# Pooled attention and a max-of-three feed-forward: batch 1's key path and steps placed elsewhere

## The chip, the cores and the metric

The kernel runs on one core of one Trainium2 chip. The metric is the device time of one launch, in microseconds. The core has engines with instruction streams of their own: TensorE (PE in the profile, its weight loads PEld), VectorE (DVE), ScalarE (ACT), GpSimd (POOL) and SyncE (SP). Each works through its own stream in the order in which the program wrote it, and they meet through semaphores. DMA transfers are started from the streams of POOL and SP here.

## The reference

```python
# q, k, v: (8, 8, 576, 64); pool = 8, Sp = 72
k_p = k.reshape(B, H, Sp, pool, D).mean(axis=3)
v_p = v.reshape(B, H, Sp, pool, D).mean(axis=3)
scores = scale * np.matmul(q, k_p.transpose(0, 1, 3, 2))
attn = softmax(scores)                         # over the 72 pooled keys
x = np.matmul(attn, v_p)                       # (8, 8, 576, 64)
x = x.transpose(0, 2, 1, 3).reshape(4608, 512)
h = np.maximum(np.maximum(x @ w1, x @ w2), x @ w3)   # w1, w2, w3: 512 x 768
out = h @ w_out                                      # 768 x 512
```

Keys and values are averaged over groups of eight positions, 576 queries of each head attend to 72 pooled keys, and the result goes through a layer that takes the largest of three products.

## The kernel before

**The arithmetic.** The maximum is taken against the first product: `h = x w1 + max(0, x (w2 - w1), x (w3 - w1))`, so `sub_w` subtracts w1 from w2 and w3 once, and `x w1 wout` becomes one product with `wm = w1 wout`, which `linear` makes once. For it w1 has to stand transposed: `turn_w(jc)` transposes one of six slabs of 128 columns on TensorE (four transposes into the PSUM buffer of the tag `tr`, of which there is one) and copies it to `w1T`.

**The blocks.** The 4608 tokens are done in nine blocks of 512 (`block(n, plan)`), eight batches of 576 tokens feed them. `hidden` makes the hidden layer of a block: for each of six slabs the product with w2-w1 (ScalarE takes the relu into `t`) and the product with w3-w1 (VectorE takes the maximum into `hT`). `project` makes the output: per 128 tokens four matmuls of `xT` with `wm` and six of `hT` with `wout`, a copy `osb` on ScalarE and two stores. In block 0 the product `linear` stands between them: four row slabs of six matmuls, copied to `wm` by VectorE and ScalarE in turn.

**The slots.** `hidden`, `linear` and `project` are generators. After each piece they yield, and `block` then writes the steps that the plan holds for that slot: so the order on TensorE is laid down by hand. Block 0 has 34 slots: 0 to 17 in `hidden`, 18 to 25 in `linear` (one after every three matmuls), 26 to 33 in `project` (an even one after the four matmuls with `wm`, an odd one after the six with `wout`). In block 1, which has no `linear`, slots 0 to 11 come after four matmuls of 256 columns each, 12 to 17 after four of 512, and 18 to 25 are those of `project`.

**The steps of a batch.** `K` or `fold_k` sums eight keys to one (`kp`, each sum twice side by side). `k` is `turn_k`: six transposes of `kp` into PSUM, then two VectorE copies (`fill_kz`) to `kz`, of which there are two, by parity of the batch. `q0` to `q3` transpose four parts of the queries through the buffer `tr` and copy them to `qT` on ScalarE (small letter) or VectorE (capital `Q`). `s0` to `s7` are the heads' scores: three matmuls into one of the two PSUM buffers of the tag `att`, then an exponential on ScalarE. `v0` to `v4` multiply 128 queries of all heads with the pooled values, in an `att` buffer, and VectorE divides. `x0` to `x4` transpose that into `xT`. `w` is `turn_w`, `d` is `sub_w`, and `T` is a DMA that transposes all queries of a batch, from batch 3 on.

**Who folds.** Batch 0's keys and values are folded on VectorE and TensorE in the prologue. From batch 1 on GpSimd folds: `fold_k(b)` halves eight keys to four, four to two, and writes the last sum twice, through a float32 buffer `half`; `fold_v(b)` does the same for the values. GpSimd's stream also starts the loads: behind all weights stand the loads of batch 1 and 2, then `fold_k(1)`, `fold_v(1)`, the loads of batch 3, `fold_k(2)`, `fold_v(2)`, and in each later block the loads of batch n+3 and the folds of batch n+2 (`pool_work`). A load into one of the two buffers of a kind waits until the batch before the last has been read.

**PSUM.** Eight banks: `tr` 1, `pw` 3, `att` 2 of two banks each. The `pw` buffers carry the hidden products, the row slabs of `linear` and the output in turn, so the fourth of a row waits for the first to be read.

**The prologue** (L374 to L450) warms TensorE up with `heat(n)`, n multiplications of 512 columns into `tr` that nobody reads. Single ones stand at L438, L441 and L445 between the last score steps of batch 0.

Of the kernel before, what the change touches and what calls it, by code (L numbers as in the profile page):

```python
# [14 lines left out]
def kernel(  # L15
# [11 lines left out]
    nc = tc.nc  # L27
    dt = mybir.dt
    F32, BF16, F16 = dt.float32, dt.bfloat16, dt.float16

    B, H, S, D = q.shape
# [19 lines left out]
    const = ctx.enter_context(tc.tile_pool(name="const", bufs=1))  # L51
# [6 lines left out]
    kts, vts, qbs, kps, qTs, ets = {}, {}, {}, {}, {}, {}  # L58
# [65 lines left out]
    nc.vector.memset(vp_all[:, :, :, D:65], float(POOL))  # L124
    xT = const.tile([128, KCH, TOK], F16, name="xT", tag="xT")

    def fold(e, t, outs):
        part, n = t.shape[:2]
        f = const.tile([part, n, 4, D], F32, name="half", tag="half")
        e.tensor_tensor(out=f, in0=t[:, :, 0:4, :], in1=t[:, :, 4:8, :], op=ALU.add)  # L130
        e.tensor_tensor(out=f[:, :, 0:2, :], in0=f[:, :, 0:2, :], in1=f[:, :, 2:4, :],  # L131
                        op=ALU.add)
        for o in outs:
            e.tensor_tensor(out=o, in0=f[:, :, 0, :], in1=f[:, :, 1, :], op=ALU.add)  # L134

    def new_kp(b):
        kps[b] = sb2.tile([96, 6, 2, D], BF16, name="kp", tag="kp")

    def fold_k(b, e, i0=0, i1=6):
        if b not in kps:  # L140
            new_kp(b)
        fold(e, kts[b][:, i0:i1], [kps[b][:, i0:i1, i, :] for i in range(2)])

    def fold_v(b):
        fold(nc.gpsimd, vts[b], [vp_all[:, b, :, 0:D]])
# [1 line left out]
    def pool_v(b, h, g, tag, evac):  # L147

        pvp = psp.tile([128, g - h, D], F32, name="pvp", tag=tag[0], bufs=tag[1])
        for j in range(POOL):  # L150
            nc.tensor.matmul(pvp, identh[0:Sp, :], vts[b][:, h:g, j, :],
                             start=(j == 0), stop=(j == POOL - 1))
        evac(out=vp_all[:, b, h:g, 0:D], in_=pvp[0:Sp])

    def turn_q(b, n0, n1, evac, tag):
        if b not in qTs:
            qTs[b] = sb2.tile([128, 2 * NG, 128], BF16, name="qT", tag="qT")
        pqt = psp.tile([128, n1 - n0, 128], BF16, name="pqt", tag=tag[0],
                       bufs=tag[1])
        qf = qbs[b].rearrange("p hp t d -> p (hp t d)")  # L160
        for n in range(n0, n1):
            nc.tensor.transpose(pqt[:, n - n0, :], qf[:, 128 * n:128 * n + 128],  # L162
                                ident)
        evac(out=qTs[b][:, n0:n1, :], in_=pqt)

    def keys(b, tag):
        pkt = psp.tile([128, 6, 96], BF16, name="pkt", tag=tag[0], bufs=tag[1])
        for i in range(6):
            nc.tensor.transpose(pkt[:, i, :], kps[b][:, i, :, :], ident[0:96, 0:96])  # L169
        return pkt  # L170

    def fill_kz(b, par, h0, h1, pkt, evac):
        rows = slice(64 * par, 64 * par + 64)
        evac(out=kz_all[b % 2][rows, par, h0:h1, 0:Sp].rearrange(  # L174
                 "p h (r i) -> p h r i", i=6),
             in_=pkt[rows, :, 12 * h0:12 * h1].rearrange("p i (h r) -> p h r i", r=12))

    def turn_k(b):
        pkt = keys(b, TR)
        for par in range(2):  # L180
            fill_kz(b, par, 0, H, pkt, nc.vector.tensor_copy)

    def pool_k(b, tag):

        new_kp(b)
        pkp = psp.tile([128, 6, D], F32, name="pkp", tag=tag[0], bufs=tag[1])
        for j in range(POOL):
            nc.tensor.matmul(pkp, identh[0:96, :], kts[b][:, :, j, :],
                             start=(j == 0), stop=(j == POOL - 1))
        nc.vector.tensor_copy(out=kps[b][:, :, 0, :], in_=pkp[0:96])  # L190
        nc.scalar.copy(out=kps[b][:, :, 1, :], in_=pkp[0:96])
# [12 lines left out]
    def new_et(b):  # L204
        ets[b] = sb2.tile([Sp, H, S], F16, name="et", tag="et")

    def scores(b, h):
        psc = psp.tile([128, 1024], F32, name="psc", tag="att", bufs=2)
        score(b, h, psc[:, 0:320], 0, 0, 5)
        score(b, h, psc[:, 320:512], 1, 0, 3)  # L210
        score(b, h, psc[:, 512:576], 1, 3, 4)
        exp(ets[b][:, h, :], psc[0:Sp, 0:S])
# [33 lines left out]
    TR = ("tr", 1)  # L246
    PW = ("pw", 3)
# [4 lines left out]
    def do(b, steps):  # L252

        for name in steps.split():
            i = int(name[1:] or 0)
            if name[0] in "qQ":
                turn_q(b, *QS[i], nc.vector.tensor_copy if name[0] == "Q"
                       else nc.scalar.copy, TR)  # L260
            elif name[0] == "T":
                qTs[b] = sb2.tile([128, 2 * NG, 128], BF16, name="qT", tag="qT")
                nc.sync.dma_start_transpose(
                    out=qTs[b], in_=qbs[b].rearrange("p hp t d -> p (hp t d)"))
            elif name[0] == "k":
                turn_k(b)
            elif name[0] == "K":
                pool_k(b, PW)
            elif name[0] == "p":
                pool_v(b, 4 * i, 4 * i + 4, TR, nc.scalar.copy)  # L270
            elif name[0] == "s":
                if i == 0:
                    new_et(b)
                scores(b, i)
            elif name[0] == "d":
                sub_w(i)
            elif name[0] == "w":
                turn_w(i, nc.scalar.copy if i % 2 else nc.vector.tensor_copy)
            elif name[0] == "v":
                xns[b, i] = values(b, CHUNKS[i][0])  # L280
            else:
                turn_x(b, *CHUNKS[i], xns[b, i], ("att", 2),
                       nc.vector.tensor_copy if name[0] == "X" else nc.scalar.copy)
# [4 lines left out]
    def sub_w(i):  # L288

        part = slice(256 * i, 256 * i + 256)  # L290
        for t in w_sb[1:]:
            nc.vector.tensor_tensor(out=t[:, :, part], in0=t[:, :, part],
                                    in1=w_sb[0][:, :, part], op=ALU.subtract)

    def turn_w(jc, evac):
        pwt = psp.tile([128, KCH, 128], F16, name="pwt", tag=TR[0], bufs=TR[1])
        for kc in range(KCH):
            nc.tensor.transpose(pwt[:, kc, :], w_sb[0][:, kc, bass.ts(jc, 128)], identh)
        evac(out=w1T[:, jc, :], in_=pwt.rearrange("p k c -> p (k c)"))
# [68 lines left out]
    def new_hT():  # L368
        return sb2.tile([128, JCH, NB], F16, name="hT", tag="hT")
# [4 lines left out]
    def heat(n):  # L374
        for _ in range(n):
            nc.tensor.matmul(wm, warm[:, 0:128], warm, start=True, stop=True)
# [4 lines left out]
    k16 = const.tile([96, 6, 4, D], F16, name="k16", tag="k16")  # L381
# [56 lines left out]
    heat(1)  # L438
    turn_x(0, 0, 0, xn0[0], PW)
    scores2(2)  # L440
    heat(1)  # L441
    turn_x(0, 128, 0, xn0[1], PW, nc.vector.tensor_copy)
    sub_w(0)
    scores2(4)
    heat(1)  # L445
    scores2(6)


# [3 lines left out]
    def block(n, plan):  # L452

        hT = new_hT()
        slot = 0
        for part in (hidden(n, hT), project(n, hT)):
            for _ in part:
                if slot == 0 and n > 0:
                    pool_work(n, mms[-1])
                for b, steps in plan.get(slot, ()):  # L460
                    if b < B:
                        do(b, steps)
                slot += 1

    fold_k(1, nc.gpsimd)
    fold_v(1)
    block(0, {0: [(0, "v2 w0")], 1: [(0, "v3 d1")], 2: [(0, "x2")],
# [8 lines left out]
    load_k(3, nc.gpsimd)  # L476
    load_v(3, nc.gpsimd)
# [5 lines left out]
    def plan1():  # L483
        return {0: [(1, "v3")], 1: [(1, "x2")], 2: [(1, "v4")], 3: [(1, "x3")],
                5: [(1, "x4")],
                6: [(2, "q0")], 8: [(2, "q1")], 9: [(2, "k")], 11: [(2, "q2 s0")],
                12: [(2, "s1 q3")], 13: [(2, "s2")], 14: [(2, "s3")], 15: [(2, "s4")],
                16: [(2, "s5")], 18: [(2, "s7")],
                19: [(2, "v0")],
                20: [(2, "v1 x0")], 21: [(2, "v2 x1")], 22: [(2, "v3 x2")],  # L490
                23: [(2, "v4 x3")], 24: [(2, "x4")], 17: [(2, "s6"), (3, "T")]}
# [52 lines left out]
```

## Time and profile before

| | |
|---|---|
| median of 3 runs | 245.76 us (244.63 to 247.13) |
| the profiled execution | 245.13 us |
| its span, first to last instruction | 243.4 us |
| share of TensorE busy | 94% |
| mean granted TensorE clock | 0.985 |
| DVE, ACT, POOL busy | 42%, 44%, 53% |
| HBM read, written | 34.60 MB, 9.44 MB |

A row of the profile's timeline reads: start, duration, engine, source line, operation, tile written <- tiles read, shapes, count; in brackets the idle time of the engine before it and what ended it. Rows that follow each other on an engine may be merged with a count. A matmul's duration includes the time until it has drained, so matmuls overlap in the rows: the pace of a stretch is read from the starts. A row of the waits reads: the instruction that waited, `<-` what it waited for, total, times and the longest. Rows of groups give the count, the union of the busy time and the mean of one in ns.

### The profile page before, as it was taken

The numbers are of one execution on the slowest core, as the hardware profiler recorded it, in microseconds if no ns is written. First come the engines' busy times: TensorE is split into PE (matmuls) and PEld (weight loads), VectorE is DVE, ScalarE is ACT, GpSimd is POOL, SyncE is SP. The second block draws the span as 40 slices with busy tenths as digits, with TensorE's granted clock in tenths as the row PEclk, the third lists the DMA queues.
The fourth block names the chain that finished last, engine by engine and source line by source line (L and its number), as shares of the span: only waits on it lengthen the run. The fifth ranks groups of instructions, "written<-read, shape, count | busy, mean of one in ns | idle before, by whom it ended". The sixth has DMA issues, their size and how long they took to land.

```text
span 243.4 us, 4167 instructions
## 1 busy us (share of the span) xinstructions
PE 227.9 (94%) x1632; PEld 124.1 (51%) x1632; DVE 101.4 (42%) x189; ACT 105.9 (44%) x184; POOL 129.0 (53%) x93
## 2 busy tenths in 40 slices
PE   7788984999989999999999999899999999999993
PEld 3466631556855645555555555355545554444442
DVE  3669734305542543454352536243633442402400
ACT  2355420464667447415813661265147413223321
POOL 8574159999809999937991999993000000000000
PEclk9999996899999999999999999999999999999999
DMA  6999999599799349997998999770452066033024
GB/s 180 204 197 196 219 196 209 92 156 227 109 211 157 89 79 177 148 209 119 200 178 186 139 216 182 141 174 21 92 129 51 3 138 131 3 85 87 0 62 113
DMA packets 47139, 33.51 MB, mean 138 GB/s; under 512 B 27344, under 2 KB 41680, under 8 KB 47120
## 3 DMA queue, kind: packets, MB, share of 16 engines
q0 software_dynamic: 16864, 16.72, 43.8%
q1 hardware_dynamic: 30096, 16.39, 33.1%
q8 instruction: 13, 0.21, 0.4%
q10 hardware_dynamic: 160, 0.13, 0.3%
q14 instruction: 6, 0.05, 0.1%
HBM read 34.60 MB, written 9.44 MB: 181 GB/s over the span
## 4 chain that ended last, share of the span: by engine, by line
PE 80%; DMA 10%; POOL 5%; DVE 2%; issue 1%; ACT 1%; POOLq 0%
PE pw L319 34%; PE po L355 19%; PE po L351 13%; DMA ktFalse<-in_k_dram 6%; PE psc L197 6%; DMA mw<-in_moe_w_dram 4%; PE pav L232 4%; PE pm L306 2%; POOL half L130 1%; DVE kz L174 1%; PE pxt L223 1%; PE pkt L169 1%; PE pqt L162 1%; POOL vt L78 1%; POOL kp L134 1%
## 5 line engine op out<-in xcount | busy, mean ns | idle before, releaser
L319 PE MATMUL pw<-xT,mw 128*128 128x512 f16 (+1 forms) x480 | 106.2, 358 | 1.4 <-ACT osb L360 0.9
L327 DVE TENSOR_TENSOR hT<-t,pw 128x512 f16<-128x512 f16 (+1 forms) x60 | 38.0, 633 | 68.6 <-PE pw L319 38.6
L319 PEld LDWEIGHTS <-mw 128*128 128x128 f16 x480 | 42.4, 98 | 35.4 <-issue 1.7
L355 PE MATMUL po<-mwo,hT 128*128 128x512 f16 (+1 forms) x222 | 52.7, 373 | 0.0
L325 ACT ACTIVATE t<-pw 128x512 f16<-128x512 f32 (+1 forms) x60 | 33.3, 555 | 32.7 <-PE pw L319 32.6
L360 ACT COPY osb<-po 128x512 f32<-128x512 f32 (+1 forms) x36 | 20.9, 579 | 61.2 <-PE po L355 61.2
L202 ACT ACTIVATE et<-psc 72x576 f16<-72x576 f32 (+2 forms) x62 | 40.6, 658 | 9.1 <-PE psc L197 9.1
L351 PE MATMUL po<-wm,xT 128*128 128x512 f16 (+1 forms) x148 | 37.1, 373 | 0.0
L355 PEld LDWEIGHTS <-hT 128*128 128x128 f16 x222 | 20.2, 98 | 19.6
L131 POOL TENSOR_TENSOR half<-half 96x768 f32<-96x768 f32 (+1 forms) x14 | 29.0, 2074 | 1.1
L130 POOL TENSOR_TENSOR half<-vt 72x2048 f32<-72x2048 f16 x7 | 28.4, 4058 | 0.6
L240 DVE TENSOR_TENSOR xn<-pav,rcp 128x512 f16<-128x512 f32 x40 | 27.6, 691 | 1.4
L197 PE MATMUL psc<-qT,kz 128*128 128x64 bf16 (+3 forms) x192 | 26.1, 246 | 0.3 <-DVE kz L174 0.3
L197 PEld LDWEIGHTS <-kz 128*128 128x128 bf16 x192 | 18.0, 98 | 15.9 <-DVE kz L174 1.4
L130 POOL TENSOR_TENSOR half<-ktFalse 96x1536 f32<-96x1536 f16 x7 | 21.7, 3099 | 7.4 <-DMA ktFalse<-in_k_dram 7.3
L174 DVE COPY kz<-pkt 64x576 bf16<-64x576 bf16 (+1 forms) x16 | 11.4, 716 | 21.9 <-PE pkt L169 21.7
L232 PEld LDWEIGHTS <-et 72*128 72x128 f16 x320 | 15.5, 98 | 8.5 <-issue 0.5
L351 PEld LDWEIGHTS <-xT 128*128 128x128 f16 x148 | 13.3, 98 | 12.6
L238 DVE RECIPROCAL rcp<-pav 128x8 f32<-128x8 f32 x40 | 8.2, 205 | 23.9 <-PE pav L232 23.7
L232 PE MATMUL pav<-vp,et 72*128 72x65 f16 x320 | 17.0, 194 | 0.4 <-ACT et L202 0.4
L134 POOL TENSOR_TENSOR kp<-half 96x384 bf16<-96x384 f32 x14 | 13.6, 991 | 0.6
L87 POOL DMA_DIRECT2D qb<-in_q_dram x9 | 7.0, 777 | 9.6 <-DMA qT<-qb 6.5
(48 smaller groups left out, 118.3 us busy)
## 6 DMA issues: line engine op xcount, KB each, us to landing
out_dram<-osb SPq DMA_DIRECT2D x70, 128.0 KB, 2.4
ktFalse<-in_k_dram POOLq DMA_DIRECT2D x7, 576.0 KB, 7.5
qb<-in_q_dram POOLq DMA_DIRECT2D x7, 576.0 KB, 15.1
vt<-in_v_dram POOLq DMA_DIRECT2D x7, 576.0 KB, 12.5
mw<-in_moe_w_dram POOLq DMA_DIRECT2D x9, 256.0 KB, 9.5
ktTrue<-in_k_dram SPq DMA_DIRECT2D x3, 384.0 KB, 5.0
mwo<-in_moe_w_out_dram POOLq DMA_DIRECT2D x1, 768.0 KB, 12.9
qb<-in_q_dram POOLq DMA_DIRECT2D x2, 288.0 KB, 7.9
```

What stands on the lines that cost most here:

```text
L130: e.tensor_tensor(out=f, in0=t[:, :, 0:4, :], in1=t[:, :, 4:8, :], op=ALU.add)
L131: e.tensor_tensor(out=f[:, :, 0:2, :], in0=f[:, :, 0:2, :], in1=f[:, :, 2:4, :], op=ALU.add)
L197: nc.tensor.matmul(out, kz_all[b % 2][:, f % 2, h, :], qTs[b][:, n + i0:n + i1, 64 * (h % 2):64 * (h % 2) + 64], start=True, stop=True)
L202: nc.scalar.activation(out=out, in_=in_, func=FT.Exp, scale=1.0 / 64.0)
L232: nc.tensor.matmul(pav[:, h // 4, 65 * (h % 4):65 * (h % 4) + 65], ets[b][:, h, c0:c0 + 128], vp_all[:, b, h, :], start=True, stop=True)
L240: nc.vector.tensor_tensor(out=xn, in0=pv[:, :, :, 0:D], in1=rcp.to_broadcast([128, 2, 4, D]), op=ALU.mult)
L319: mm = nc.tensor.matmul(pw, w_sb[wi][:, kc, bass.ts(jc, 128)], xT[:, kc, col], start=(kc == 0), stop=(kc == KCH - 1))
L325: nc.scalar.activation(out=t, in_=pw, func=FT.Relu)
L327: nc.vector.tensor_tensor(out=hT[:, jc, c0:c1], in0=t, in1=pw, op=ALU.max)
L351: nc.tensor.matmul(po, xT[:, kc, bass.ts(m, 128)], wm_sb[:, kc, c], start=(kc == 0), stop=False)
L355: nc.tensor.matmul(po, hT[:, jc, bass.ts(mm, 128)], wo_sb[:, jc, c], start=False, stop=(jc == JCH - 1))
L360: nc.scalar.copy(out=osb[:, c], in_=po)
```

## The change

Batch 1's keys are no longer folded by GpSimd ahead of block 0 but by VectorE in slot 17 of block 0, with a buffer of type float16 for the half sums (`k16`, which batch 0's fold has used before). Batch 1's query and key steps, which stood in slots 18 to 24, inside `linear`, stand behind it, from slot 24 on, and its eight score steps in slots 26 to 30 in place of 22 to 30. Query part 0, 1 and 2 of batch 1 are copied by ScalarE, which VectorE did. The first two transposes of w1 take the place of two single warm-up multiplications in the prologue, and the other four move up. The key transposes of all batches from 1 on go into an `att` buffer instead of `tr`, and in block 1 batch 2's key step comes ahead of its first query step. The step letter `K`, which no plan had used, calls `fold_k` on VectorE in place of `pool_k`.

```diff
-    def fold(e, t, outs):
+    def fold(e, t, outs, dtype=F32):
         part, n = t.shape[:2]
-        f = const.tile([part, n, 4, D], F32, name="half", tag="half")
+        f = const.tile([part, n, 4, D], dtype, name="half" if dtype == F32 else "halfh",
+                       tag="half" if dtype == F32 else "k16")
         e.tensor_tensor(out=f, in0=t[:, :, 0:4, :], in1=t[:, :, 4:8, :], op=ALU.add)
...
-        fold(e, kts[b][:, i0:i1], [kps[b][:, i0:i1, i, :] for i in range(2)])
+        fold(e, kts[b][:, i0:i1], [kps[b][:, i0:i1, i, :] for i in range(2)],
+             F16 if e is nc.vector else F32)
...
     def turn_k(b):
-        pkt = keys(b, TR)
+        pkt = keys(b, ("att", 2))
...
             elif name[0] == "K":
-                pool_k(b, PW)
+                fold_k(b, nc.vector)
...
     scores2(2)
-    heat(1)
+    turn_w(0, nc.scalar.copy)
     turn_x(0, 128, 0, xn0[1], PW, nc.vector.tensor_copy)
     sub_w(0)
     scores2(4)
-    heat(1)
+    turn_w(1, nc.vector.tensor_copy)
     scores2(6)
...
-    fold_k(1, nc.gpsimd)
     fold_v(1)
-    block(0, {0: [(0, "v2 w0")], 1: [(0, "v3 d1")], 2: [(0, "x2")],
-              3: [(0, "x3 w1")], 4: [(0, "v4")], 6: [(0, "x4")],
-              8: [(0, "w2")], 9: [(0, "w3 d2")], 12: [(0, "w4")], 13: [(0, "w5")],
-              19: [(1, "k")],
-              18: [(1, "Q0")], 20: [(1, "Q1")], 22: [(1, "Q2 s0")], 23: [(1, "s1")],
-              24: [(1, "Q3")],
-              25: [(1, "s2")], 26: [(1, "s3")], 27: [(1, "s4")], 28: [(1, "s5")],
-              29: [(1, "s6")], 30: [(1, "s7")], 31: [(1, "v0")],
+    block(0, {0: [(0, "v2")], 1: [(0, "v3 d1")], 2: [(0, "x2")],
+              3: [(0, "x3 w2")], 4: [(0, "v4")], 6: [(0, "x4")],
+              8: [(0, "w3")], 9: [(0, "d2")], 12: [(0, "w4")], 13: [(0, "w5")],
+              17: [(1, "K")], 24: [(1, "q0 k")], 25: [(1, "q1")],
+              26: [(1, "s0 q2")], 27: [(1, "s1 s2")], 28: [(1, "s3 Q3")],
+              29: [(1, "s4 s5")], 30: [(1, "s6 s7")], 31: [(1, "v0")],
               32: [(1, "v1 x0")], 33: [(1, "X1 v2")]})
...
-                6: [(2, "q0")], 8: [(2, "q1")], 9: [(2, "k")], 11: [(2, "q2 s0")],
+                6: [(2, "k")], 8: [(2, "q0")], 9: [(2, "q1")], 11: [(2, "q2 s0")],
```

## The prediction

> **What bounds the kernel now.** I read the page first, then the waits of TensorE, then the chain that ended last, then the timelines of the stretch to which these point.
>
> ```profile
> span 243.4 us, 4167 instructions
> ...
> PE 227.9 (94%) x1632; PEld 124.1 (51%) x1632; DVE 101.4 (42%) x189; ACT 105.9 (44%) x184; POOL 129.0 (53%) x93
> ...
> PE pkt L169 <- POOL kp L134: 3.0, 1, 3.0
> ...
> PE pqt L162 <- DVE kz L174: 1.1, 2, 0.7
> ...
> PE pkt L169 <- ACT qT L164: 0.3, 1, 0.3
> ```
>
> TensorE is the bound: 94% of the span. What it does not fill is little, and the list of its waits says where it lies: the longest is that of the key transposes (`pkt`) for GpSimd's folded keys, and the other two shown, like a fourth that the timeline below has, belong to the key and query steps of batches 1 and 2. The chain names the same place.
>
> ```profile
> 17.70 15.06 DMA ktFalse<-in_k_dram
> ...
> 32.84 3.09 POOL half L130
> ...
> 37.88 1.95 POOL kp L134 x2
> ```
>
> Batch 1's keys are loaded until 32.84, and GpSimd then folds for 7 us, to 39.83. Up to the load the chain is made of transfers, behind it of matmuls. Now TensorE in that stretch, with the granted clock of two windows of 5 us around it.
>
> ```profile
> 34.01 0.81 PE L306 MATMUL pm<-mwo,w1T 128*128 128x512 f16 x3
> 35.81 0.45 PE L162 MATMUL pqt<-ident,qb 128*128 128x128 bf16 x5 [0.99 <-DMA qb<-in_q_dram]
> ...
> 39.87 0.66 PE L169 MATMUL pkt<-ident,kp 96*128 96x96 bf16 x6 [2.96 <-POOL kp L134]
> ...
> 42.15 0.71 PE L162 MATMUL pqt<-ident,qb 128*128 128x128 bf16 x5 [0.34 <-DVE kz L174]
> ...
> 45.00 0.39 PE L162 MATMUL pqt<-ident,qb 128*128 128x128 bf16 x4
> 45.22 0.41 PE L197 MATMUL psc<-qT,kz 128*128 128x320 bf16 x3
> 45.47 0.81 PE L306 MATMUL pm<-mwo,w1T 128*128 128x512 f16 x3
> 46.12 0.41 PE L197 MATMUL psc<-qT,kz 128*128 128x320 bf16 x3
> ...
> 48.13 1.03 PE L351 MATMUL po<-wm,xT 128*128 128x512 f16 x4
> ...
> 35.00:40.00 5.00, 1.23 (x10) 0.63 (x11) 1.18 (x2) 0.00 (x0) 4.75 (x5) 0.79 1.25 207
> 40.00:45.00 5.00, 4.66 (x21) 2.00 (x20) 2.00 (x3) 0.58 (x1) 4.92 (x2) 0.52 0.97 175
> ```
>
> The stage `linear` runs from 34.01 to 48.13, 14.12 us. Its work at full pace is read from the starts: three matmuls of 512 columns take 0.65 (45.47 to 46.12), four transposes 0.22 (45.00 to 45.22), a head's scores 0.25 (45.22 to 45.47). The stage holds 24 matmuls (5.20), 18 query transposes and 6 key transposes (1.32) and three heads of scores (0.75): 7.27 us. So 6.85 us are lost here. The waits in brackets are 4.29 of them; the rest, 2.56, is half speed: TensorE, which had done 1.23 us of work in the window before, has a granted clock of 0.52 from 40 to 45. The gain to be had is these 6.85, not the wait of 3.0.
>
> **The change part by part.** *Keys of batch 1 on VectorE.* GpSimd loses 7 us of work, but gets nothing done earlier.
>
> ```profile
> 20.39 0.85 POOL L78 DMA_DIRECT2D vt<-in_v_dram  x1 [0.18 <-issue]
> ...
> 39.91 4.04 POOL L130 TENSOR_TENSOR half<-vt 72x2048 f32<-72x2048 f16 x1
> ...
> vt<-in_v_dram POOLq DMA_DIRECT2D x1, 576.0 KB, 19.4
> ```
>
> Its next task, the fold of batch 1's values at 39.91, began as their load landed (issued at 20.39, 19.4 to landing: 39.8). So I let all later GpSimd work stand where it is. VectorE pays for the keys.
>
> ```profile
> 34.27 0.69 DVE L327 TENSOR_TENSOR hT<-t,pw 128x512 f16<-128x512 f16 x1 [1.04 <-PE pw L319]
> ...
> L292 DVE TENSOR_TENSOR mw<-mw,mw 128x1024 f16<-128x1024 f16 x6 | 3.9, 683 | 0.0
> L386 DVE TENSOR_TENSOR k<-ktTrue 96x512 f16<-96x512 f32 x3 | 2.1, 685 | 2.8 <-DMA ktTrue<-in_k_dram 2.8
> L202 ACT ACTIVATE et<-psc 72x576 f16<-72x576 f32 x56 | 36.0, 642 | 7.3 <-PE psc L197 7.3
> L360 ACT COPY osb<-po 128x512 f32<-128x512 f32 x35 | 20.5, 585 | 60.7 <-PE po L355 60.7
> ```
>
> Four additions of 1536, 768, 384 and 384 columns, 3072 in all. Both rows of VectorE take 0.68 us, one for 1024 columns with everything in 16 bits, one for 512 from float32. By the first the fold takes 3072 / 1024 x 0.683 = 2.05, and some more for four starts: 2.2. By the second it takes 3072 / 512 x 0.685 = 4.1. All operands have 16 bits, so I take 2.2 and keep 4.1. It starts when VectorE has finished the last maximum (34.27 + 0.69 = 34.96; the keys have landed at 32.84) and ends at 37.2. Queued behind it is VectorE's copy of the first `wm` slab, of 128x512 like the maximum, so 0.69, to 37.9. Who waits for that: the fourth slab of `linear`, which needs the first one's PSUM buffer, at 34.01 + 3 x 1.30 = 37.9. So about 0.1; with 4.1 for the fold it is 1.8 to 1.9. From below: nothing.
>
> *Steps behind the product.* Key transposes come 21 matmuls into `linear`, at 34.01 + 7 x 0.65 = 38.6: after the fold (37.2) and after the queries (35.8). So the 0.99, the 2.96 and the half clock that follows them all go, and the key transposes in `att` leave `tr` to the queries, so the 0.34 goes. What is late next is ScalarE. The scores share three slots two by two, and with two `att` buffers a head waits for the exponential of the last but one. Slots 29 and 30 hold four heads: TensorE has four matmuls, six, and four heads (0.86 + 1.30 + 1.00 = 3.2 us), ScalarE four exponentials and one output copy (4 x 0.642 + 0.585 = 3.2). They are level, so each hiccup becomes a wait. I take 0.7 over all slots, an estimate of one exponential; nothing at the least, and at most two exponentials (1.3), one for each crowded slot of the last two.
>
> *The first value step.* It needs the pooled values of batch 1 and comes at 55.84 now, some 6 us earlier then, about 50. GpSimd is done with them at 46.45 + 1.27 = 47.7. Nothing.
>
> ```profile
> 55.84 0.42 PE L232 MATMUL pav<-vp,et 72*128 72x65 f16 x8
> ...
> 46.45 1.27 POOL L134 TENSOR_TENSOR vp<-half 72x512 f16<-72x512 f32 x1
> ...
> 17.81 0.38 PE L376 MATMUL wm<-warm 128*128 128x512 bf16 x1
> ...
> 17.36 1.93 ACT L202 ACTIVATE et<-psc 72x640 f16<-72x640 f32 x3
> ```
>
> *Transposes of w1 in the prologue.* Two warm-up matmuls (0.22 each at full pace) go, six transposes stay, so TensorE has 0.43 less. Against it: ScalarE's three exponentials end at 19.29, and a copy like `osb` (0.585) now stands among them; the second transpose waits for that copy, as `tr` is one buffer, and batch 0's third value step for the last exponential. VectorE gets one copy more ahead of the value steps. I take 0.15 later for the start of `linear`, between 0.3 earlier and 0.6 later.
>
> *Block 1.* The key step ahead of the queries, outside `tr`, removes the wait of 0.34 for the ScalarE copy and the longer one of the two for `kz`, 0.75. But the first two query steps are now one slot apart, as the second and the keys were, and that cost 0.34: I take 0.4, at most 0.9. Net 0.7.
>
> *Later blocks.* The key step's buffer is read before the first score needs it, so nothing. The sum: 6.85 - 0.1 - 0.7 - 0.15 + 0.7 = 6.6 us. From 245.13 for the profiled execution (span 243.4 and 1.7 around it) that is **238.5**; the median of the three runs, 245.76, lies 0.6 higher, and the range allows for it.
>
> **Where GpSimd may become the bound.**
>
> ```profile
> 59.72 0.60 PE L319 MATMUL pw<-xT,mw 128*128 128x256 f16 x4 [0.25 <-DVE xT L227]
> ...
> 64.07 0.44 PE L162 MATMUL pqt<-ident,qb 128*128 128x128 bf16 x5
> ...
> 88.28 0.42 PE L169 MATMUL pkt<-ident,kp 96*128 96x96 bf16 x6
> ...
> 54.90 1.95 POOL L134 TENSOR_TENSOR kp<-half 96x384 bf16<-96x384 f32 x2
> ...
> 72.61 0.78 POOL L87 DMA_DIRECT2D qb<-in_q_dram  x1 [6.50 <-DMA qT<-qb]
> ...
> 78.46 1.94 POOL L134 TENSOR_TENSOR kp<-half 96x384 bf16<-96x384 f32 x2
> ...
> 63.77 3.58 SPq L263 DMA_TRANSPOSE qT<-qb  x1
> ...
> 89.45 10.51 SPq L263 DMA_TRANSPOSE qT<-qb  x1
> ```
>
> Batch 2's keys are wanted in block 1's slot 6, where the query step at 64.07 stands, 4.35 after the block's start at 59.72; with the block 5.9 earlier that is 58.2, and they are folded at 56.85. Batch 3's are wanted at 88.28 - 6.6 = 81.7 and folded at 80.40. Both margins are 1.3. So GpSimd caps the gain at 88.28 - 80.40 = 7.9.
>
> **The rivals.**
> - *The fold at float32 pace.* For it: its last outputs change type, and its rows are short strided pieces. Against it: the row of 1024. Its 1.7 more give 240.2; with the scores' upper bound 240.8.
> - *GpSimd caps.* If no new wait shows, the gain would be 8.2 (6.85, block 1's 1.1, the prologue's 0.3), and the key step of batch 3 holds it at 7.9: 237.3.
> - *The clock at the start of block 0.* Transposes replace warm-up matmuls at 17 to 18 us. If the clock falls there as it did at 40, that costs what five us at 0.52 cost there, 2.4, and 240.9 results. Against it, in the stretch that is already rich in transposes and small matmuls, TensorE keeps its clock:
>
> ```profile
> 10.00:15.00 5.00, 4.25 (x57) 3.51 (x54) 2.80 (x8) 3.31 (x5) 2.96 (x4) 1.00 1.36 198
> ```
>
>   The Trainium skill speaks for this rival: "TensorE: Matmul & The Clock Gate", Part 4: PE-mode transpose, says that transposes do not count as busy for the clock in the same way as matmuls. By that rule the two steps would bring the stretch nearer to a drop; the row above does not bear it out, and I keep it at a small chance.
> - *Slower: the transposing DMA of batch 3.* GpSimd waits 6.50 for it ahead of a load at 72.61, and batch 3's fold stands behind that load. It takes SyncE 3.58 at 63.77, the next of its kind 10.51. Stores and loads meet otherwise when TensorE runs ahead; if this one takes 6.9 longer, the keys come at 87.3, TensorE waits 5.6 at the start of block 2 and, as at 40, runs at half clock afterwards (2.4): 8.0 lost against 6.6 gained, 246.5. It decides from 5.5 us longer on (1.3 of margin, 6.6 - 2.4 of waiting). Against it: its load starts at the same time as now, and block 0's stores get out of its way.
> - *The change doesn't do what it says:* the waits move on instead, to the pooled values or the keys of batch 2, and some 244 remains. Against it stand the margins of 2 and 1.3 us.
>
> **How the numbers follow.** My forecast, all parts as in the sum: 0.55. Fold or scores at their upper bounds: 0.2. GpSimd caps: 0.1. Clock: 0.06. Slower DMA: 0.04. Nothing gained: 0.05. The range: its low end is the cap of 7.9 with half a microsecond for the runs' scatter, 236.8; its high end takes the fold's and the scores' upper bounds (2.3) and the 0.6 to the median, 241.4. Beyond it lie the last two cases and part of the clock's, with what I may have missed some 2 in 10. A measurement tells about 1% from no change: faster 0.91 (the first four), within 1% 0.05 (nothing gained), slower 0.04 (the DMA).
>
> **What would show it.** Right: no wait of `pkt` for GpSimd; a granted clock of 1.0 from 35 to 45; `linear` as 24 matmuls in 5.2 to 5.4 us; block 1 at about 54; the four additions on VectorE 2.2 us together; block 2's keys without a wait. Wrong: a wait of the fourth slab for `wm`, of scores for exponentials over 1.3, or of key transposes in blocks 1 or 2 for GpSimd.

## The result, and the profile after

The changed kernel takes 237.82 us (median of 4 runs, 237.35 to 246.42), the kernel before 245.19 beside it; the ratio, which leaves the execution of 246.42 out, is 0.9679, 95% interval 0.9619 to 0.9739. The profiled execution is that of 246.42: it lost 9 us in a single place, which a later section takes up; the other three lie between 237.35 and 238.17. So the profile of a second set of runs of the same kernel is shown here (237.49 us; experiment 1).

First its waits of TensorE, the whole list:

```profile
PE wm L378 <- DVE warm L102: 1.5, 1, 1.5
PE pw L321 <- DMA xT<-xn: 1.4, 1, 1.4
PE pkp L393 <- DVE k L388: 0.9, 1, 0.9
PE pxt L225 <- DVE xn L242: 0.9, 3, 0.4
PE pav L234 <- ACT et L204: 0.6, 2, 0.5
PE pwt L300 <- ACT w1T L301: 0.6, 1, 0.6
PE pqt L164 <- ACT qT L166: 0.3, 1, 0.3
PE psc L199 <- DVE kz L176: 0.3, 1, 0.3
PE pw L321 <- DVE xT L229: 0.3, 1, 0.3
```

The waits of the key transposes for GpSimd, of the queries for their load and for the key copies are gone. What is new is a wait of 0.6 in the prologue (`pwt` for ScalarE's copy), 0.3 of a query step for ScalarE, and 1.4 for a transposing DMA, late in the kernel. Now the stage that had lost 6.85 us, from TensorE's timeline and two windows (busy time of PE, PEld, DVE, ACT, POOL, then the granted clock):

```profile
33.33 4.70 PE L308 MATMUL pm<-mwo,w1T 128*128 128x512 f16 x21
37.87 0.44 PE L164 MATMUL pqt<-ident,qb 128*128 128x128 bf16 x5
38.15 0.42 PE L171 MATMUL pkt<-ident,kp 96*128 96x96 bf16 x6
38.40 0.81 PE L308 MATMUL pm<-mwo,w1T 128*128 128x512 f16 x3
39.09 0.44 PE L164 MATMUL pqt<-ident,qb 128*128 128x128 bf16 x5
39.36 1.03 PE L353 MATMUL po<-wm,xT 128*128 128x512 f16 x4
...
46.52 0.94 PE L199 MATMUL psc<-qT,kz 128*128 128x320 bf16 x6
47.31 1.46 PE L357 MATMUL po<-mwo,hT 128*128 128x512 f16 x6
...
52.48 0.60 PE L321 MATMUL pw<-xT,mw 128*128 128x256 f16 x4 [0.25 <-DVE xT L229]
...
79.26 1.03 PE L321 MATMUL pw<-xT,mw 128*128 128x512 f16 x4
```

```profile
35.00:40.00 5.00, 5.00 (x37) 2.67 (x35) 3.99 (x8) 2.03 (x4) 0.77 (x1) 1.00 1.23 212
40.00:45.00 5.00, 5.00 (x38) 2.92 (x37) 0.57 (x2) 3.82 (x7) 4.92 (x2) 1.00 1.03 191
```

All 24 matmuls of `linear` follow each other, interrupted only by transposes that need not wait, TensorE is busy for the whole of both windows, and the clock, 0.52 before, is 1.00. The two heads at 46.52 take 0.79 to the next row, where two heads without a wait take 0.5: that is all that the packing of the scores costs.

Laid against the 245.13 us of the profile before, stage by stage from the starts: `linear` begins 0.68 earlier (33.33 for 34.01); from there to block 1 it is 19.15 us for 25.71, 6.56 less; block 1 takes 26.78 for 27.70, 0.92 less. Together 8.16. Behind that 0.5 is given back, for the rest takes 156.4 (235.7 - 79.26) for 156.0 (243.4 - 87.42).

### The profile page after: what moved, and what is told of

Its sections match the earlier page's. It is cut to its first block, busy times and chain, and to the rows that moved or that the text cites. A ratio compares the mean times of both kernels' runs of the same rounds, so it can differ in the third digit from the quotient of the medians.

```text
span 244.6 us, 4167 instructions
## 1 busy us (share of the span) xinstructions
PE 226.3 (93%) x1629; PEld 123.9 (51%) x1630; DVE 101.6 (42%) x190; ACT 107.3 (44%) x187; POOL 122.2 (50%) x89
## 4 chain that ended last, share of the span: by engine, by line
PE 83%; DMA 9%; DVE 3%; issue 1%; ACT 1%; POOL 1%; POOLq 0%; DVEq 0%
PE pw L321 38%; PE po L357 17%; PE po L353 12%; DMA xT<-xn 6%; PE psc L199 6%; PE pav L234 4%; DMA vt<-in_v_dram 3%; PE pm L308 2%; PE pxt L225 2%; DVE mw L294 1%; DVE xn L242 1%; PE pkt L171 1%; PE pqt L164 1%; PE pvp L153 1%; POOL qb L87 0%
## 5 line engine op out<-in xcount | busy, mean ns | idle before, releaser
L321 PE MATMUL pw<-xT,mw 128*128 128x512 f16 (+1 forms) x480 | 108.3, 363 | 7.8 <-DMA xT<-xn 7.6
L321 PEld LDWEIGHTS <-mw 128*128 128x128 f16 x480 | 43.0, 99 | 43.2 <-DMA xT<-xn 7.1
L132 POOL TENSOR_TENSOR half<-half 72x1024 f32<-72x1024 f32 (+1 forms) x13 | 27.2, 2096 | 1.0
L353 PEld LDWEIGHTS <-xT 128*128 128x128 f16 x148 | 13.3, 98 | 12.6
L131 POOL TENSOR_TENSOR half<-ktFalse 96x1536 f32<-96x1536 f16 x6 | 18.6, 3104 | 0.1
L72 POOL DMA_DIRECT2D ktFalse<-in_k_dram x7 | 3.9, 557 | 19.9 <-PE pw L321 11.9
L135 POOL TENSOR_TENSOR kp<-half 96x384 bf16<-96x384 f32 x12 | 11.7, 992 | 0.5
## 6 DMA issues: line engine op xcount, KB each, us to landing
qb<-in_q_dram POOLq DMA_DIRECT2D x7, 576.0 KB, 14.8
```

The costliest lines, as they stand in the source:

```text
L321: mm = nc.tensor.matmul(pw, w_sb[wi][:, kc, bass.ts(jc, 128)], xT[:, kc, col], start=(kc == 0), stop=(kc == KCH - 1))
L353: nc.tensor.matmul(po, xT[:, kc, bass.ts(m, 128)], wm_sb[:, kc, c], start=(kc == 0), stop=False)
```

## The experiments

The changed kernel ran again in the first set of experiments at 237.17 (ratio to before 0.9683, 0.9656 to 0.9710); what follows is compared with that. Theory A is the prediction's: the wait and the half clock behind it go because the steps stand where their data have arrived. Theory B: the gain is the work taken off GpSimd. Theories C, D and E are about the execution of 246.42.

**1. The changed kernel again.** No edit.

> The changed kernel as it is, profiled again. Theory A (the 246.4 of its first profiled execution is one wait of 6.6 us for transposing DMAs at the start of block 3, with half clock behind it, and no property of the change's steps in blocks 0 and 1): about 237.5, no wait of more than 1 us behind 60 us, and the same pace as before in blocks 0 and 1 (block 1 begins at 52.5, block 2 at 79.3). Theory C (the change always meets this collision when it is profiled): again 246, with 6 us of waiting for xT at 102.

Measured 236.75 to 237.87, ratio 0.9683 (0.9656 to 0.9710), and no wait at the start of block 3. Blocks 0 and 1 ran at the same pace as in the profile of 246.42 (block 1 at 52.53 there and 52.48 here, block 2 at 79.31 and 79.26). So C falls: those 9 us were lost behind block 2's start.

**2. The change without the fold.** GpSimd folds batch 1's keys, as before; all else, the key transposes in `att` and the prologue too, stays as the change has it.

```diff
+    fold_k(1, nc.gpsimd)
     fold_v(1)
...
-              17: [(1, "K")], 24: [(1, "q0 k")], 25: [(1, "q1")],
+              24: [(1, "q0 k")], 25: [(1, "q1")],
```

> The changed kernel with one part undone: GpSimd folds batch 1's keys, as before; the steps stay behind the product. Theory A (the order takes the wait off TensorE, the fold on VectorE only shortens what is left): the keys are ready at 39.8, the key step comes at 38.2, so a wait of 1.6 and no half clock: 1.6 over the changed kernel, 239.3. Theory B (taking 7 us of folding off GpSimd is what gains): most of the gain is gone, 244 to 245.

238.62, ratio 0.9748 (0.9716 to 0.9780). TensorE's timeline:

```profile
38.09 0.44 PE L164 MATMUL pqt<-ident,qb 128*128 128x128 bf16 x5
39.72 0.43 PE L171 MATMUL pkt<-ident,kp 96*128 96x96 bf16 x6 [1.19 <-POOL kp L135]
39.99 0.81 PE L308 MATMUL pm<-mwo,w1T 128*128 128x512 f16 x3
```

The keys come where they came before, at 39.7; only TensorE waits 1.2 us for them in place of 3.0, and the three matmuls behind take 0.65 to the next start: the clock holds. Of 8 us this part of the change brings 6.6: 5.2 in the stage (block 1 begins at 54.07, so 20.51 us for 25.71), the rest in block 1 and the prologue. B falls. The order without the new place of the key transposes was not run by itself.

**3. The fold alone.** VectorE folds in slot 17, all steps stay inside the product as before. The edits that give `fold` its type and `K` its new meaning are those of the change and not shown again.

```diff
-    fold_k(1, nc.gpsimd)
     fold_v(1)
...
-              19: [(1, "k")],
+              17: [(1, "K")], 19: [(1, "k")],
```

> The kernel before with one part of the change: VectorE folds batch 1's keys in slot 17 in float16; all steps stay inside the product. Theory A: the keys are ready at 37, but the first query step still waits 1 us for its load, its copy on VectorE stands behind the fold, and the key step waits about 1 for the one buffer of the transposes and the next query step 1 for the key copies; 3 us of waiting in place of 4.3, with or without half clock: 241.5 to 243.5. Theory B: all of the gain, 237.5 to 238.5.

241.13, ratio 0.9842 (0.9804 to 0.9881): about half of the gain, and a little less time than theory A had. From TensorE's timeline and windows of 2 us:

```profile
35.08 0.45 PE L164 MATMUL pqt<-ident,qb 128*128 128x128 bf16 x5 [0.84 <-DMA qb<-in_q_dram]
...
36.96 0.41 PE L171 MATMUL pkt<-ident,kp 96*128 96x96 bf16 x6 [0.78 <-DVE qT L166]
...
38.99 0.67 PE L164 MATMUL pqt<-ident,qb 128*128 128x128 bf16 x5 [0.97 <-DVE kz L176]
```

```profile
36.00:38.00 2.00, 1.23 (x10) 0.55 (x9) 2.00 (x5) 0.00 (x0) 0.00 (x0) 1.00 1.23 209
38.00:40.00 2.00, 1.03 (x8) 0.74 (x8) 1.22 (x3) 0.00 (x0) 1.04 (x1) 0.77 1.19 214
40.00:42.00 2.00, 2.00 (x6) 0.64 (x5) 0.19 (x1) 0.58 (x1) 2.00 (x1) 0.50 1.15 222
```

The keys are in time, but three waits are left, for the queries' load, for a copy queued behind the fold, and for the one transposing buffer: all matters of where the steps stand. That is 2.6 us of waiting, and in this execution (242.26) half clock once more, though none of the waits reaches 1 us. The other three executions, 240.06 to 241.28, have a mean granted clock of 1.000, where this one has 0.993.

**4. The prologue as before.**

```diff
-    turn_w(0, nc.scalar.copy)
+    heat(1)
...
-    turn_w(1, nc.vector.tensor_copy)
+    heat(1)
...
-    block(0, {0: [(0, "v2")], 1: [(0, "v3 d1")], 2: [(0, "x2")],
-              3: [(0, "x3 w2")], 4: [(0, "v4")], 6: [(0, "x4")],
-              8: [(0, "w3")], 9: [(0, "d2")], 12: [(0, "w4")], 13: [(0, "w5")],
+    block(0, {0: [(0, "v2 w0")], 1: [(0, "v3 d1")], 2: [(0, "x2")],
+              3: [(0, "x3 w1")], 4: [(0, "v4")], 6: [(0, "x4")],
+              8: [(0, "w2")], 9: [(0, "w3 d2")], 12: [(0, "w4")], 13: [(0, "w5")],
```

> The changed kernel with the prologue and the w1 transposes as before. Theory A: linear began at 34.01 before and at 33.38 after; part of these 0.6 us is the edit: 0.3 to 0.6 slower than the changed kernel, 238.0. The prediction's own step (0.15 in the edit's disfavour) would have it 0.15 faster.

237.70, ratio 0.9695 (0.9665 to 0.9725): not to be told from the changed kernel. In its profile `linear` begins at 33.61, 0.28 later than in experiment 1's, and block 1 at 52.76 for 52.48. As far as two profiles can say, the edit gains 0.3.

**5, 6. The fold in float32.** First with the buffer `half` in place of `k16`, then with the memory of batch 0's keys, which nobody reads any more:

```diff
-             F16 if e is nc.vector else F32)
+             F32)                                                  # 5
...
+             kts[0][:, :, 0:4, :] if e is nc.vector else None)     # 6, as the buffer f
```

> The changed kernel with the fold on VectorE through the float32 buffer. Theory A (what makes the fold harmless is that it is done before the fourth slab needs the first one's buffer): the fold takes 3.5 to 4.1 in place of 2.1, ends at 38, the copy of the first wm slab at 38.7, the fourth slab waits 1.3 to 1.8 for it: 238.5 to 239. If VectorE's fold has slack: 237.2, no wait.

251.89, ratio 1.0265 (1.0199 to 1.0330): slower than before the change, where 238.5 to 239 were expected. VectorE's timeline, from the last maximum on, says why:

```profile
33.52 0.69 DVE L329 TENSOR_TENSOR hT<-t,pw 128x512 f16<-128x512 f16 x1 [1.04 <-PE pw L321]
47.07 1.75 DVE L131 TENSOR_TENSOR half<-ktFalse 96x1536 f32<-96x1536 f16 x1 [12.86 <-POOL vp L135]
```

There is one buffer `half` (its first addition is shown), and GpSimd's fold of the values stands ahead in the program: so the fold waited 12.86 us for work that it doesn't need, and TensorE 12.70 for the keys. My expectation had missed that the change's float16 buffer is also another buffer.

> The changed kernel with the half sums of batch 1's keys in float32, but in the memory of batch 0's keys, which are no longer read, and not in the buffer that GpSimd's folds use. In the run before, with the shared buffer, VectorE's fold waited until 47 for GpSimd's fold of the values; its four additions took 3.7 us. If that wait was all of the 14 us lost there: the additions start at 34 and end at 37.9, the first wm copy at 38.6, the fourth slab waits 1.3 us for it, no other wait: 1.3 over the changed kernel, 238.5 to 239. If float32 itself costs more than that: 241 and up.

238.40, ratio 0.9692 (0.9660 to 0.9725), in a set in which the kernel before took 245.89: no difference from the changed kernel can be told.

```profile
34.27 1.75 DVE L131 TENSOR_TENSOR ktTrue<-ktFalse 96x1536 f32<-96x1536 f16 x1
36.05 0.95 DVE L132 TENSOR_TENSOR ktTrue<-ktTrue 96x768 f32<-96x768 f32 x1
37.04 1.02 DVE L135 TENSOR_TENSOR kp<-ktTrue 96x384 bf16<-96x384 f32 x2
37.98 1.28 DVE L312 CAST wm<-pm 128x512 f16<-128x512 f32 x2
```

```profile
33.39 4.70 PE L308 MATMUL pm<-mwo,w1T 128*128 128x512 f16 x21
...
40.77 0.29 PE L199 MATMUL psc<-qT,kz 128*128 128x192 bf16 x2 [0.19 <-DVE kz L176]
```

The timelines of VectorE and TensorE: the fold took 3.7 us for 2.1, but the fourth slab of `linear` (from matmul 19 on, at 37.3) ran before VectorE had copied the first (37.98): the wait of 1.3 on which I had counted does not exist. Of the three buffers only that of the second slab had been read by then, by ScalarE (36.18 to 36.77). The slower fold shows at the first score alone, in a named wait of 0.19; the stage takes 19.51 us (33.39 to 52.90) for 19.15.

**7. The keys in `tr`.** The key transposes back in that buffer, and block 1 in its old order.

```diff
-        pkt = keys(b, ("att", 2))
+        pkt = keys(b, TR)
...
-                6: [(2, "k")], 8: [(2, "q0")], 9: [(2, "q1")], 11: [(2, "q2 s0")],
+                6: [(2, "q0")], 8: [(2, "q1")], 9: [(2, "k")], 11: [(2, "q2 s0")],
```

> The changed kernel with the key transposes in the buffer tr again and block 1's order as before. Theory A: in block 0 the key transposes wait 0.9 for ScalarE's copy of the first queries and the second queries 1.3 for the key copies; in block 1 the waits of 0.34 and 0.75 come back for the 0.34 that is there now: 2.2 + 0.75 over the changed kernel, 240. If the placement only matters in block 1, as the step of the prediction that gave it 0.34 in block 0 nearly had it: 238.

240.50, ratio 0.9773 (0.9756 to 0.9789). Four waits in TensorE's timeline:

```profile
39.28 0.41 PE L171 MATMUL pkt<-ident,kp 96*128 96x96 bf16 x6 [0.78 <-ACT qT L166]
...
41.31 0.45 PE L164 MATMUL pqt<-ident,qb 128*128 128x128 bf16 x5 [0.97 <-DVE kz L176]
...
61.52 0.41 PE L171 MATMUL pkt<-ident,kp 96*128 96x96 bf16 x6 [0.34 <-ACT qT L166]
...
63.55 0.40 PE L164 MATMUL pqt<-ident,qb 128*128 128x128 bf16 x4 [0.74 <-DVE kz L176]
```

So the buffer is the third part of the gain, some 2 us in block 0 (33.52 to 54.72, 21.20 us for 19.15), without which the new order would wait on itself.

**The execution of 246.42.** In its trace TensorE ends block 2 on time and then stands still:

```profile
100.56 1.46 PE L357 MATMUL po<-mwo,hT 128*128 128x512 f16 x6
108.66 1.86 PE L321 MATMUL pw<-xT,mw 128*128 128x512 f16 x4 [6.64 <-DMA xT<-xn]
```

```profile
108.00:110.00 2.00, 1.34 (x4) 0.54 (x5) 0.00 (x0) 0.00 (x0) 0.00 (x0) 0.50 0.76 215
```

6.64 us for batch 3's transposing DMAs, and half clock behind: the 9 us. The DMAs had taken 9.9 us to land (median of five), 2.5 in experiment 1. From 86 to 98 us the DMA engines moved 84 GB/s, 174 in experiment 1. Two streams meet there: the transposing DMA of batch 4's queries (SP) and the loads of batch 5 (POOL). The first two rows are of the execution of 246.42, from the timelines of SP and of POOL, the next two the same of experiment 1:

```profile
81.34 1.95 SPq L265 DMA_TRANSPOSE qT<-qb  x1
```

```profile
81.78 0.56 POOL L72 DMA_DIRECT2D ktFalse<-in_k_dram  x1
```

```profile
81.29 1.91 SPq L265 DMA_TRANSPOSE qT<-qb  x1
```

```profile
82.55 0.56 POOL L72 DMA_DIRECT2D ktFalse<-in_k_dram  x1
```

With 0.44 us between the two, the transpose took 19.4 to land and the load of batch 5's queries 24.3; with 1.26 between them 6.5 and 13.1. Before the change the transpose began behind the load (89.45 and 88.75), and batch 3's transposes came only at 102. Three experiments moved these two.

**8. Loads late in block 2.**

```diff
-                if slot == 0 and n > 0:
+                if slot == (6 if n == 2 else 0) and n > 0:
                     pool_work(n, mms[-1])
```

> The changed kernel with one change: in block 2 the loads of batch 5 start in slot 6 (about 87 us), not as soon as GpSimd is free (82 to 82.5), so that the transposing DMA of batch 4's queries, issued at 81.3, is done first. Theory D (the 246.4 comes from these two starting within half a microsecond of each other, after which all their transfers and the transposes behind them crawl): the transposing DMA lands within 5 us, batch 3's transposes in 2 to 4, block 3 starts without a wait, 237 in every run. Theory E (something else disturbed that execution): no difference from the changed kernel, 237, but the transposing DMA takes 6.5 as in its undisturbed profile.

238.45, ratio 0.9714 (0.9648 to 0.9781). The transposing DMA lands in 4.0, as D has it, but block 3 waits 1.2 us for batch 3's transposes: the later loads are now still under way when these begin. Half a miss for D.

**9, 10. Both held back**, the transpose to two matmuls ahead of the loads, first in slot 4, then in slot 8 of block 2. `every` lists all hidden matmuls as `mms` does the last of each group; the numbers are those of slot 4.

```diff
-                if slot == 0 and n > 0:
+                if slot == (4 if n == 2 else 0) and n > 0:
...
-                nc.sync.dma_start_transpose(
+                turn = nc.sync.dma_start_transpose(
                     out=qTs[b], in_=qbs[b].rearrange("p hp t d -> p (hp t d)"))
+                if b == 4:
+                    after([turn], every[-3])
...
-        got[9].append((b + 1, "T"))
+        got[4 if n == 2 else 9].append((b + 1, "T"))
```

> The changed kernel with the transposing DMA of batch 4 and the loads of batch 5 both held back in block 2, the transpose to two matmuls (0.43 us) ahead of the loads. Theory D: the transposing DMA lands after some 19 us, batch 3's transposes take 10, TensorE waits for them some 6 us at the start of block 3, with half clock behind it: 243 to 248 in most runs. Theory E: 237.

237.47, ratio 0.9676 (0.9615 to 0.9738): the two didn't meet, since GpSimd was late by itself (its loads began at 86.04, the transpose at 84.44), because the transposing DMA of batch 3 took 7.1 us this time. It tells nothing about D.

> The changed kernel with the transposing DMA of batch 4 and the loads of batch 5 both held back to slot 8 of block 2, where GpSimd is surely free, the transpose two matmuls (0.43 us) ahead. In the try in slot 4 GpSimd came 1.6 us behind and the transpose landed in 3.9. Theory D: the transpose takes over 10 us to land, batch 3's transposes 10, and TensorE waits for them over 5 us at the start of block 3: 243 to 248. Theory E: below 239.

244.99 (six runs, 242.93 to 246.00), ratio 0.9939 (0.9907 to 0.9970). The timelines of SP, POOL and TensorE and a window:

```profile
89.00 1.86 SPq L265 DMA_TRANSPOSE qT<-qb  x1
```

```profile
89.70 0.56 POOL L72 DMA_DIRECT2D ktFalse<-in_k_dram  x1 [7.25 <-PE psc L199]
```

```profile
108.09 1.86 PE L323 MATMUL pw<-xT,mw 128*128 128x512 f16 x4 [5.66 <-DMA xT<-xn]
```

```profile
108.00:112.00 4.00, 3.91 (x15) 1.71 (x16) 1.50 (x2) 0.60 (x1) 1.75 (x3) 0.50 1.11 283
```

The six executions lose some 6 to 9 us against experiment 1, and the profiled one shows the wait of the 246.42 and the same half clock. That is not what E had forecast. But the query transpose itself landed in 7.5, not over 10: so D's mechanism is too narrow. What orders these profiles is the landing of batch 5's last load (its issue plus its time to land), for batch 3's first transpose lands at about that time:

```text
kernel                      last load   batch 3's first transpose   block 3
                            lands       issued       lands          waits
experiment 1                 97.1        94.1         97.6           0
slot 4 (experiment 9)       100.5        94.5        101.0           0.34 (put down to issue)
late loads (8)              101.1        94.1        101.4           1.20
slot 8 (10)                 107.4        94.6        105.1           5.66
execution of 246.42         107.5        94.2        107.5           6.64
```

Block 3 wants batch 3's transposes at 101.8, and here they land late while the loads run. In 10 the loads are late because they start late; in the execution of 246.42 they started early and were slow, and the wait is of the same kind. Why they were slow stays open. That the half microsecond decides rests on that one execution, for no other profile has so short a gap. In those with the loads 0.70 to 1.53 us behind batch 4's transpose, it took 6.3 to 7.5 to land. With the loads 0.36 to 0.71 ahead of it, it took 16.4 to 18.2, but the last load no more than 14.8 to 16.5; 24.3 is seen once. That something else disturbed this execution, theory E, is not ruled out.

**11. Loads late in all blocks.**

```diff
-                if slot == 0 and n > 0:
+                if slot == (6 if n > 1 else 0) and n > 0:
```

> As the late loads of block 2, but in all later blocks too. Theory D: each batch's transposing DMA goes ahead of the next loads, none takes SyncE 10 us, and the wait of 1.4 us for transposes at 147 goes too: 235.5 to 236.5. If GpSimd then folds too late, waits for the keys at the start of blocks 4 to 6 and no gain.

241.36, ratio 0.9815 (0.9737 to 0.9893): a miss. No transposing query DMA takes SyncE 10 us any more, but the wait for `xT` at the start of a later block grows (3.1 us at 151; 1.4 at 148 in experiment 1), as 8 and 10 would have it, and block 3 waits 1.0 us, put down to an output copy. Nothing found here beats the changed kernel.

**12. The kernel before, again.**

> The kernel before, profiled again, for the scatter of the prologue: if linear begins at 34.0 again, the 0.68 us by which it began earlier in the changed kernel are an effect of the edit, less the 0.28 that the undone prologue showed; if it begins between 33.4 and 33.7, as with the old prologue in two experiments, half of them are scatter.

246.16 for the profiled execution. `linear` begins at 33.76, between the two cases, so 0.25 us between two profiles of one kernel is scatter. It waits 3.1 for the keys as in the first profile, and its clock stays low for longer: 0.54 from 40 to 44 and 0.61 from 44 to 48. So the half clock's price varies between executions.

## Why the prediction was right, and where its steps were not

*The stage, 6.85 less 0.8.* Right in kind and size: 6.56 measured. Both halves are shown: no wait of `pkt`, and a clock of 1.00 from 35 to 45. Of the causes, the order with the key transposes out of `tr` brings 5.2 of the stage's 6.56 (experiment 2), some 2 of them by that buffer (7); the fold on VectorE is worth the rest, and alone about 4 of the whole 8 (3).

*The fold, 2.2 us.* 2.11 measured (0.94 + 0.55 + 0.62), so the row of 1024 columns was the right one. The upper end was wrong, though: "the fourth slab of `linear`, which needs the first one's PSUM buffer" did not wait in experiment 6, where the fold took 3.7. That step, like the description of the kernel ahead of it, took the three `pw` buffers to go round in turn. What the fold must beat is the key step at 38.15; it ends at 36.4, 1.8 us ahead.

*ScalarE late next, 0.7.* The size was 0.3, at the last two heads alone. The mechanism fits but is argued: `s7` starts at 47.06, as ScalarE's exponential of `s5` (0.65 from 46.37) ends, and the profile names no wait there.

*The prologue, 0.15 against the change.* Its wait came as foreseen (0.6 for ScalarE's copy), but `linear` began 0.68 earlier, not later. In all the profiles together it begins at 33.43 to 34.01 with the old prologue (four, mean 33.7) and at 33.15 to 33.79 with the new (ten, mean 33.4): some 0.3 is the edit, the rest scatter, and so luck. Against the forecast the prologue was 0.8 better, the stage 0.5, block 1 0.2, the later blocks 0.5 worse: that is the way from 238.5 to the 237.49 of experiment 1.

*Block 1, 0.7.* 0.92; the new wait of 0.34 between the query steps is there to the hundredth.

*"I let all later GpSimd work stand where it is."* This step failed, though not by the change. GpSimd's fold of the values did start with the landing of its load, as said. But the transposing DMA of batch 3, for which GpSimd had waited 6.50 us, landed in 4.0 us for 8.3, and batch 3's keys were folded at 74.7, not 80.4. The first two rows are of experiment 1; the next three, of the kernel before in experiment 12, show the same without the change:

```profile
66.90 0.78 POOL L87 DMA_DIRECT2D qb<-in_q_dram  x1 [1.45 <-DMA qT<-qb]
...
72.76 1.95 POOL L135 TENSOR_TENSOR kp<-half 96x384 bf16<-96x384 f32 x2
```

```profile
67.25 0.78 POOL L87 DMA_DIRECT2D qb<-in_q_dram  x1 [1.58 <-DMA qT<-qb]
...
73.11 1.95 POOL L134 TENSOR_TENSOR kp<-half 96x384 bf16<-96x384 f32 x2
...
89.51 0.56 POOL L72 DMA_DIRECT2D ktFalse<-in_k_dram  x1 [6.55 <-PE pkt L169]
```

The wait of 6.50 was that of one execution, and the cap on the gain, 7.9, which rested on it, was none. What the change does move is the start of batch 5's loads. In the kernel before they wait for TensorE's key transposes of batch 3 (last row; 88.75 in the first profile); with TensorE 8 us ahead they start as soon as GpSimd is free, 6 us earlier, next to a transposing DMA that had come forward by 8. It cost the forecast nothing in the usual case, but it made the meeting that the last part of the experiments is about.

*Later blocks, nothing.* 0.5 given back, a wait for transposing DMAs (1.41 us at 148) in place of one for an output copy (0.86 at 156).

*The slower rival* had the right kind of event, a transposing DMA that collides when TensorE runs ahead, with half clock behind it, and the wrong place: it expected batch 3's queries and the start of block 2. It was batch 3's attention output and block 3, at 9 us in place of 8.

*The clock in the prologue.* It did not fall. The window is of the execution of 246.42, in which the two steps stand too:

```profile
15.00:20.00 5.00, 3.62 (x52) 2.93 (x52) 4.21 (x9) 3.64 (x7) 2.42 (x4) 1.00 1.45 197
```

What the Trainium skill, "TensorE: Matmul & The Clock Gate", Part 4: PE-mode transpose, says of transposes and the clock brought no loss here.

## What to carry to other kernels

Price a wait of TensorE with the half clock behind it, and ask first whether the waiting step can stand later, where its data have come anyway: with another buffer for the step that brought 5.2 of the stage's 6.6 us here. When work moves between engines, look at the buffers that it shares with its old neighbours; a scratch buffer left in common cost 14 us. And when TensorE moves ahead by some us, list the transfers that keep their own time: they now meet others, and a rare meeting does not show in a median. Before a wait in one profile is taken for a bound, profile the same kernel twice: the 6.50 us here were 1.58 the next time.

## What the hardware showed that was not expected

The clock can fall without a long gap, and the same waits do not bring it down every time. In the profiled execution of experiment 3 no wait reaches 1 us, but TensorE was busy for 1.23 and 1.03 us of two successive windows of 2 us, and the clock went to 0.77 and 0.50. The other three executions of that kernel have a mean clock of 1.000. In the profile of experiment 7 two waits of 0.78 and 0.97 left it at 1.00, but two other executions of that kernel have a mean of 0.996 and 0.993; where it fell there is not on record. What decides is not shown. The Trainium skill, "TensorE: Matmul & The Clock Gate", Why this matters for your kernels, advises against idle gaps above some 3 us. By that rule experiment 3 would have kept its clock; the measurement of its profiled execution differs.

A transposing DMA between two on-chip buffers that was issued while plain loads were in flight landed about when the last of them did. In experiment 1, in the execution of 246.42 and in experiments 2, 8, 9 and 11 batch 3's first one landed 0 to 1.1 us behind the last load of batch 5, 3.5 to 13.3 us after its issue; in experiment 10, after 10.5 us, 2.3 ahead of it. Those issued behind that landing took 2.3 to 2.8.
